# The last two VectorE instructions of a rational activation change places, and one output copy moves up in ScalarE's order

## The chip, the cores and the metric

The kernel runs on one core of a Trainium2 chip. The metric is the device time of one execution in microseconds (us). The five engines of the core are named as in the profile: PE is TensorE's matmul, PEld its weight load, DVE is VectorE, ACT is ScalarE, POOL is GpSimd, and SP (SyncE) issues the DMAs. SBUF is the working memory. [...]

## The reference

Three stages follow each other, all in float32.

```python
# 1. attention with a decaying state, for 4 batches and 8 heads, 768 steps, head size 48
state = alpha[t][:, None] * state + outer(k[t], v[t]);  y[t] = q[t] @ state
# 2. first MoE layer: 3072 tokens, 384 -> 2048 -> 384
h = x @ w_in
P = a[0] + a[1]*h + a[2]*h**2 + a[3]*h**3
Q = 1.0 + |b[0]|*|h| + |b[1]|*h**2
x = (P / (Q + 1e-6)) @ w_out
# 3. second MoE layer, same sizes
h = x @ w_in;  out = (h * cos(h)) @ w_out
```

The change lies in the activation P / (Q + 1e-6) of stage 2, and in the copy that takes attention's output y out of PSUM.

## The kernel before

Attention works in 24 units (6 chunks of 128 time steps by 4 batches), one unit a slot. The first MoE layer is cut into 6 blocks of 512 tokens (`TB`) and 16 slices of 128 hidden channels, so 96 steps `n`; the second layer follows in the same numbering from step 96 on. From slot 20 (`LEAD`) to slot 24 a slot holds one unit of attention and then one step of the layers: `attention(n)`, then `layers(n - LEAD)`, then `y_out(n - 1)`, the copy of attention's output on ACT (line 425). After slot 24 `layers` runs alone.

The whole program stands in a manual schedule: every engine takes its instructions in the order in which the code issues them, and waits only for data and for buffers. A step of `layers(n)` issues these things. `gemm1(n)` (line 562) makes h in a PSUM bank by nine matmuls of 128x512; four banks take turns, so step n needs the bank of step n - 4. `rational(n)` then works on four older steps at once. `second(n)` is `gemm2(n - 5)` (line 578), nine matmuls of 128x512 that read the activation as two parts, `hi` and `lo`.

Inside `rational(n)`, by the age of the step that is worked on:

- step n - 4 (`four`): ACT rounds g to `hi` (line 608), POOL subtracts, lo = g - hi (line 613).
- step n - 2 (`two`): DVE goes on with the numerator, g = (g + a) h (line 628); h is in the PSUM bank. Later ACT writes the logarithm and the exponential of the denominator, thus its reciprocal's first guess r, into the same bank (lines 645 and 646).
- step n - 3 (`three`): DVE runs three instructions. Line 631 makes z = (z + 1.000001) r from SBUF and PSUM. Line 632 writes the corrected r = (z - 2/s) r back into the PSUM bank (the Newton step). Line 633 makes g = (g + c) r from SBUF and PSUM. After line 633 the bank is free for `gemm1`.
- step n - 1 (`one`): ACT makes |h| (line 636) and a h + b (line 637), POOL makes z in two instructions (line 638 with one input in SBUF, line 639 with two), DVE multiplies g by h (line 640).

Beside this, weights and tokens are split into a rounded part and a rest: POOL's line 225 (the rest of a weight), DVE's lines 77 and 78 (weight words), ACT's line 702 and DVE's line 706 (the tokens of the next block, three steps per block; line 706 has both its inputs in SBUF). In DVE's other instructions of the layer one input lies in PSUM.

Of the kernel before, what the change touches and what calls it, by code (L numbers as in the profile page):

```python
# [15 lines left out]
ALU = mybir.AluOpType  # L16
# [15 lines left out]
LN_S = 2.0 ** -22  # L32
# [10 lines left out]
def attn_then_two_moe(ctx, tc, kqT, aT, vP, w1i, w1o, ma, mb, w2i, w2o, out):  # L43
    nc = tc.nc
# [100 lines left out]
    LEAD = NU - 4  # L145
# [268 lines left out]
    def y_out(u):  # L414
        d = U[u]
        if u in late:
            d["yo"] = wp.tile([128, HP, C], F32, tag=late[u], name="yo")
        elif u < NU - B:
            d["yo"] = kept[2 + u % 2]
            if 2 <= u < B:  # L420
                d["yo"] = y_rest[:, (2 + u) * TB:(3 + u) * TB].bitcast(F32).rearrange("p (a t) -> p a t", a=HP)
        else:
            d["yo"] = in_p.tile([128, HP, C], F32, tag="p", name="yo")
        out = d["yo"].bitcast(F32R) if u < B else d["yo"]
        nc.scalar.activation(out=out, in_=d["y"], func=AF.Copy)
# [160 lines left out]
    def acc_out(most=NK):  # L586

        while outs and most:
            most -= 1
            m, blk, f, k = outs.pop(0)  # L590
            ks = slice(k * 128, (k + 1) * 128)
            if f < NF - 1:
                nc.scalar.activation(out=part(blk, k), in_=acc[k], func=AF.Copy)
                continue
            o = temp("z" if k == 1 else "g") if m or blk == NC - 1 else in_p.tile([128, TB], F32, tag="p", name="o")
            if in_parts(m, blk):
                nc.vector.tensor_tensor(out=o, in0=part(blk, k), in1=acc[k], op=ALU.add)
            elif m == 1 and k == 1 and blk in (0, NC - 1):
                nc.vector.tensor_copy(o, acc[k])
            else:  # L600
                nc.scalar.activation(out=o, in_=acc[k], func=AF.Copy)
            to = xd[1][blk, ks, :] if m == 0 else out[ks, blk * TB:(blk + 1) * TB]
            nc.sync.dma_start(out=to, in_=o)

    def round_g(n):
        t = T[n]
        t["hi"] = temp("hi", F32R)
        nc.scalar.activation(out=t["hi"], in_=t["g"], func=AF.Copy)  # L608
# [3 lines left out]
        t["lo"] = temp("lo", F32R)  # L612
        eng.tensor_tensor(out=t["lo"], in0=t["g"], in1=t["hi"].bitcast(F32), op=ALU.subtract)  # L613

    def rational(n):

        def tile_at(i):
            return T[i] if 0 <= i < N1 else None

        one, two, three, four = (tile_at(n - i) for i in range(1, 5))  # L620
        acc_out(1)
        if four:
            round_g(n - 4)
            rest_g(n - 4, nc.gpsimd)
        acc_out()
        if two:
            g = two["g"]
            nc.vector.scalar_tensor_tensor(g, g, cq[:, 3:4], two["h"], ALU.add, ALU.mult)  # L628
        if three:
            z, r, g = three["z"], three["h"], three["g"]  # L630
            nc.vector.scalar_tensor_tensor(z, z, ONE_EPS, r, ALU.add, ALU.mult)  # L631
            nc.vector.scalar_tensor_tensor(r, z, -2.0 / LN_S, r, ALU.add, ALU.mult)
            nc.vector.scalar_tensor_tensor(g, g, cq[:, 2:3], r, ALU.add, ALU.mult)  # L633
        if one:
            h, ah, g, zz = one["h"], temp("ah"), temp("g"), temp("z")
            nc.scalar.activation(out=ah, in_=h, func=AF.Abs)  # L636
            nc.scalar.activation(out=g, in_=h, func=AF.Identity, scale=cq[:, 5:6], bias=cq[:, 4:5])  # L637
            nc.gpsimd.tensor_scalar(zz, ah, cq[:, 1:2], cq[:, 0:1], ALU.mult, ALU.add)  # L638
            nc.gpsimd.tensor_tensor(out=zz, in0=zz, in1=ah, op=ALU.mult)  # L639
            nc.vector.tensor_tensor(out=g, in0=g, in1=h, op=ALU.mult)  # L640
            one.update(z=zz, g=g)
        if two:

            r = two["h"]
            nc.scalar.activation(out=r, in_=two["z"], func=AF.Ln, scale=LN_S, bias=lnb)  # L645
            nc.scalar.activation(out=r, in_=r, func=AF.Exp, scale=-1.0)

    def cosine_parts(n):

        if N1 <= n - 3 < F0:  # L650
            round_g(n - 3)
            rest_g(n - 3, nc.gpsimd)
# [572 lines left out]
        nc.vector.tensor_scalar(bad, tot, 128.0 * 2 * NU - 0.5, None, ALU.is_lt)  # L1225


    def layers(n):
        slot[0] = n + LEAD
        gemm1(n)  # L1230
        if n == F0 - 12:
            all_ok0()
        if n == F0 - 8:
            all_ok1()
        m, r = divmod(n, N1)
        blk, f = divmod(r, NF)
        nxt = (m, blk + 1) if blk + 1 < NC else (m + 1, 0)
        at, load = f - 11, f == 8
        if n < NF:
            nxt, at, load = (0, 1), n - 5, n == 3  # L1240
        elif n < 2 * NF:
            at, load = n - 2 * NF + 4, n == 2 * NF - 6
        split = 0 <= at < NK and nxt[0] < 2 and nxt != (1, 2)
        rational(n)
        cosine_parts(n)
        cosine(n)
        w_hi()
        if split:
            x_hi(*nxt, at)
        second(n)  # L1250
        if 0 < n <= NU - KEEP:
            y_store(KEEP + n - 1)
        if n:
            w_fetch(2 * NF if n < 2 * NF else 3 * NF + NO if n < N1 - NF else 4 * NF)
        if nxt != (1, 2) and load:
            for kk in range(NK):
                x_load(*nxt, kk)
        if split:
            x_lo(*nxt, at)
        i = n - (N1 - NF)  # L1260
        if n < 2 * NF:
            if n > 1:
                tick(2 if n > 4 else 1, 1)
        elif n < N1 - NF:
            if not split:
                tick(1, 1)
        elif n < N1:
            if i > 3:
                tick(1, 1)
        else:  # L1270
            tick(3 if n > N1 + 3 else 1, 1)
        if 0 <= i < NF:
            w_load(i)
        if 0 <= i - 6 < NO:
            w_load(NF + i - 6)
        w_lo([nc.gpsimd])
        if n >= N1:
            now[0] = n - N1 - NF
            prepare(*(SPLIT if split and nxt != (1, 2) else EARLY if now[0] < 0 else PLAIN))
# [7 lines left out]
    with tc.manual_schedule():  # L1287
        nc.scalar.preload_act_table_set("natural_log_exp_and_others")
        for name, u in (("a", 0), ("kq", 0), ("a", 1), ("a", 2), ("kq", 1)):
            load(u, name)  # L1290
        nc.vector.memset(fresh, P_MIN)
        nc.gpsimd.memset(ones, 1.0)
        nc.gpsimd.memset(half_pi, HALF_PI)
        nc.gpsimd.memset(lnb, LN_S * ONE_EPS)
        for t in v_t:
            nc.gpsimd.memset(t[:, H * D:], 0.0)
        nc.gpsimd.memset(ident, 1.0)
        nc.gpsimd.affine_select(
            ident, ident, pattern=[[1, 128]], compare_op=ALU.is_equal, fill=0.0, base=0, channel_multiplier=-1
        )  # L1300
        for s in s_all:
            nc.gpsimd.memset(s[:, HP * D:], 0.0)
        warm_up(13)
        x_pieces = [p for kk in range(NK) for p in x_load(0, 0, kk)]
        for n in range(-3, NU + 1):
            slot[0] = n
            if n == -1:
                load(3, "a")
                load(1, "v")
            if 0 <= n - 2 < KEEP:  # L1310
                y_store(n - 2)
            if 0 <= n - 3 < B:
                y_store(n - 3, True)
            if n >= -1:
                load(n + 5, "a")
            if n >= 0:
                load(n + 3, "kq")
                for i in range(SOME[n] if n <= LEAD else 0):
                    w_fetch(2 * NF)
                load(n + 2, "v")  # L1320
            if n == 3:
                nc.sync.dma_start(out=cab[:, 0:4], in_=ma.unsqueeze(0).to_broadcast([128, 4]))
                nc.sync.dma_start(out=cab[:, 4:6], in_=mb.unsqueeze(0).to_broadcast([128, 2]))
            if n == 6:
                nc.scalar.activation(out=cq[:, 0:2], in_=cab[:, 4:6], func=AF.Abs)
                nc.scalar.activation(out=cq[:, 2:6], in_=cab[:, 0:4], func=AF.Copy, scale=-LN_S * LN_S)
            if n >= 8 and x_pieces:
                x_pieces.pop(0)()
            if n == 1:
                warm_up(8)  # L1330
            attention(n)
            if n == -3:
                for name, u in (("v", 0), ("kq", 2)):
                    load(u, name)
            w_lo([nc.gpsimd])
            if n >= LEAD:
                layers(n - LEAD)
                y_out(n - 1)
        for n in range(NU + 1 - LEAD, F0):
            layers(n)  # L1340
        for k in range(SLOTS):
            threes(k)
        acc_out()
# [183 lines left out]
```

## Time and profile before

| what | value |
|---|---|
| median of 3 runs | 914.39 us (913.3 to 915.9) |
| profiled execution | 913.8 us, its span 912.1 us |
| granted TensorE clock | 0.996 |
| PE busy | 892.4 us (98%) |
| DVE, ACT, POOL busy | 693.9, 697.1, 702.9 us (76 to 77%) |
| attention with layers (slots 20 to 24) | about 98 to 125 us of the span |
| first MoE layer alone | about 125 to 520 us |

"Busy" is time in which an instruction of the engine runs, waits inside an instruction included. Successive instructions of one engine overlap by some hundredths of a microsecond in the records, so the busy time of a full engine comes out slightly above what it occupies.

### The profile page before, as it was taken

What the parts mean: (1) busy time and instruction counts of PE and PEld (TensorE: products, weight loads), DVE (VectorE), ACT (ScalarE), POOL (GpSimd) and SP (SyncE); (2) the same over time, 40 slices, a digit from 0 to 9 for tenths busy, and PEclk for the clock granted to TensorE, in tenths of its full rate; (3) what the DMA queues carried; (4) which work ended last, traced back from release to release, by engine and by line L of the source; (5) the groups of instructions that cost most, each with busy time, mean ns of one, the idle gap of its engine ahead of it and who ended that gap; (6) DMA issues with size and microseconds to landing.
All of it is one profiled execution on the core that took longest, in us unless ns stands there. A gap on an engine that the chain in (4) does not pass through costs nothing.

```text
span 912.1 us, 16494 instructions
## 1 busy us (share of the span) xinstructions
PE 892.4 (98%) x5732; PEld 741.2 (81%) x5732; DVE 693.9 (76%) x1247; ACT 697.1 (76%) x1302; POOL 702.9 (77%) x699
## 2 busy tenths in 40 slices
PE   7999999999999999999999999999999999999997
PEld 7788777887788888888888888878888888888885
DVE  7989799998999989989979767666366554555552
ACT  5999898989889788888788778656577666666653
POOL 6899998999889888889879668669787475655332
PEclk9999999999999999999999999999999999999999
DMA  8999545211233141232165276630243433533432
GB/s 281 357 366 370 191 124 196 82 63 36 104 107 94 57 142 45 87 107 94 53 205 185 95 238 239 202 110 27 74 134 109 161 113 96 167 102 105 139 105 90
DMA packets 67307, 128.87 MB, mean 141 GB/s; under 512 B 6928, under 2 KB 30224, under 8 KB 67216
## 3 DMA queue, kind: packets, MB, share of 16 engines
q1 hardware_dynamic: 67216, 127.74, 43.1%
q8 instruction: 47, 0.77, 0.4%
q14 instruction: 44, 0.36, 0.1%
HBM read 95.21 MB, written 32.51 MB: 140 GB/s over the span
## 4 chain that ended last, share of the span: by engine, by line
PE 72%; DVE 8%; ACT 7%; POOL 6%; DMA 4%; issue 2%; SPq 0%; DVEq 0%; ACTq 0%
PE acc L578 22%; PE b L562 18%; PE acc L1054 15%; PE b L1019 6%; PE r L1019 5%; PE r L562 4%; POOL kq L323 2%; POOL kq L318 2%; DMA kq<-kqT 2%; DVE g L628 1%; DVE z L631 1%; ACT b L645 1%; DVE g L640 1%; DMA a<-aT 1%; PE b L1198 1%
## 5 line engine op out<-in xcount | busy, mean ns | idle before, releaser
L578 PE MATMUL acc<-hi,w 128*128 128x512 f32 x738 | 252.5, 396 | 0.0
L562 PE MATMUL b<-x,w 128*128 128x512 f32 x927 | 233.8, 397 | 1.3 <-DVE g L633 1.1
L613 POOL TENSOR_TENSOR lo<-g,hi 128x512 fp32r<-128x512 f32 x128 | 170.2, 1330 | 66.2 <-ACT hi L608 59.4
L562 PEld LDWEIGHTS b<-x,w 128*128 128x128 f32 x927 | 173.4, 188 | 45.4 <-DVE g L633 4.1
L578 PEld LDWEIGHTS acc<-hi,w 128*128 128x128 f32 x738 | 138.7, 188 | 33.9
L1111 POOL TENSOR_TENSOR lo<-g,hi 128x512 fp32r<-128x512 f32 x64 | 83.0, 1297 | 103.6 <-ACT hi L1110 91.6
L578 PE MATMUL acc<-lo,w 128*128 128x512 f32 x369 | 145.7, 395 | 0.0
L639 POOL TENSOR_TENSOR z<-z,ah 128x512 f32<-128x512 f32 x96 | 124.7, 1299 | 8.0
L1054 PE MATMUL acc<-hi,w_out 128*128 128x512 f32 x384 | 130.3, 395 | 0.0
L608 ACT ACTIVATE hi<-g 128x512 fp32r<-128x512 f32 x128 | 80.4, 628 | 47.8 <-PE acc L578 32.6
L578 PEld LDWEIGHTS acc<-lo,w 128*128 128x128 f32 x369 | 69.4, 188 | 16.5
L638 POOL TENSOR_SCALAR z<-ah,cq 128x512 f32<-128x512 f32 x96 | 74.4, 775 | 5.5 <-ACT ah L636 5.4
L1054 PE MATMUL acc<-lo,w_out 128*128 128x512 f32 x192 | 76.4, 398 | 0.4 <-POOL lo L1111 0.2
L1054 PEld LDWEIGHTS acc<-hi,w_out 128*128 128x128 f32 x384 | 68.7, 188 | 9.9
L640 DVE TENSOR_TENSOR g<-g,b 128x512 f32<-128x512 f32 x72 | 49.1, 682 | 16.2 <-ACT g L637 16.0
L636 ACT ACTIVATE ah<-b 128x512 f32<-128x512 f32 x72 | 42.8, 594 | 19.9 <-PE b L562 19.6
L562 PE MATMUL r<-x,w 128*128 128x512 f32 x225 | 56.8, 397 | 1.0 <-DVE g L633 1.0
L1096 DVE SCALAR_TENSOR_TENSOR ah<-z,b 128x512 f32<-128x512 int32 x44 | 30.2, 685 | 35.9 <-ACT z L1092 35.9
L637 ACT ACTIVATE g<-b,cq 128x512 f32<-128x512 f32 x72 | 56.1, 779 | 0.0
L633 DVE SCALAR_TENSOR_TENSOR g<-g,cq,b 128x512 f32<-128x512 f32 x72 | 53.9, 748 | 2.5
L628 DVE SCALAR_TENSOR_TENSOR g<-g,cq,b 128x512 f32<-128x512 f32 x72 | 53.4, 742 | 0.5
L645 ACT ACTIVATE b<-z,lnb 128x512 f32<-128x512 f32 x72 | 50.1, 696 | 4.7 <-DVE g L628 4.0
(202 smaller groups left out, 2028.7 us busy)
## 6 DMA issues: line engine op xcount, KB each, us to landing
w_out<-wd SPq DMA_DIRECT2D x64, 384.0 KB, 3.1
kq<-kqT SPq DMA_DIRECT2D x24, 512.0 KB, 6.6
w<-wd SPq DMA_DIRECT2D x16, 384.0 KB, 3.1
wd<-w SPq DMA_DIRECT2D x16, 384.0 KB, 2.6
a<-aT SPq DMA_DIRECT2D x23, 258.0 KB, 5.8
raw<-w2o SPq DMA_DIRECT2D x14, 384.0 KB, 3.9
v<-vP SPq DMA_DIRECT2D x24, 192.0 KB, 6.6
x<-x1d SPq DMA_DIRECT2D x18, 256.0 KB, 4.2
```

The costliest lines, as they stand in the source:

```text
L562: nc.tensor.matmul(h, ws[0][f][:, w, ks], x[:, xx, kk, :], start=i == 0, stop=i == 8)
L578: nc.tensor.matmul(acc[k], ws[1][f][:, w, ks], d[g], start=first and i == 0, stop=last and i == 2)
L608: nc.scalar.activation(out=t["hi"], in_=t["g"], func=AF.Copy)
L613: eng.tensor_tensor(out=t["lo"], in0=t["g"], in1=t["hi"].bitcast(F32), op=ALU.subtract)
L628: nc.vector.scalar_tensor_tensor(g, g, cq[:, 3:4], two["h"], ALU.add, ALU.mult)
L638: nc.gpsimd.tensor_scalar(zz, ah, cq[:, 1:2], cq[:, 0:1], ALU.mult, ALU.add)
L639: nc.gpsimd.tensor_tensor(out=zz, in0=zz, in1=ah, op=ALU.mult)
L640: nc.vector.tensor_tensor(out=g, in0=g, in1=h, op=ALU.mult)
L645: nc.scalar.activation(out=r, in_=two["z"], func=AF.Ln, scale=LN_S, bias=lnb)
L1019: nc.tensor.matmul(tile[:, half], w[p], x[q], start=start and i == 0, stop=True, skip_group_check=True)
L1054: nc.tensor.matmul(acc[k], item["w"][:, w, ks], item[g], start=first, stop=last)
L1111: nc.gpsimd.tensor_tensor(out=p["lo"], in0=p["g"], in1=p["hi"].bitcast(F32), op=ALU.subtract)
```

## The change

The Newton factor is no longer multiplied into r in PSUM. Line 632 now makes g = (g + c) r with the uncorrected r, and line 633 multiplies the correction in: g = (z - 2/s) g. The product is the same up to rounding. Line 632 is now the last instruction that reads the bank, and line 633 has both its inputs, z and g, and its output in SBUF.

`layers` and `rational` take an argument `between`, which is called after the instructions on step n - 1 and in front of those on step n - 2 (the logarithm). In slots 20 to 24 `y_out` is passed there; before, it stood behind the whole of `layers`.

```diff
-    def rational(n):
+    def rational(n, between=None):
...
             nc.vector.scalar_tensor_tensor(z, z, ONE_EPS, r, ALU.add, ALU.mult)
-            nc.vector.scalar_tensor_tensor(r, z, -2.0 / LN_S, r, ALU.add, ALU.mult)
             nc.vector.scalar_tensor_tensor(g, g, cq[:, 2:3], r, ALU.add, ALU.mult)
+            nc.vector.scalar_tensor_tensor(g, z, -2.0 / LN_S, g, ALU.add, ALU.mult)
...
             one.update(z=zz, g=g)
+        if between:
+            between()
         if two:
...
-    def layers(n):
+    def layers(n, between=None):
...
-        rational(n)
+        rational(n, between)
...
             if n >= LEAD:
-                layers(n - LEAD)
-                y_out(n - 1)
+                layers(n - LEAD, partial(y_out, n - 1))
```

## Rows read from the trace of the kernel before

**Rows 1.** Page, part 1: busy time, share of the span, instructions.
```profile
PE 892.4 (98%) x5732; PEld 741.2 (81%) x5732; DVE 693.9 (76%) x1247; ACT 697.1 (76%) x1302; POOL 702.9 (77%) x699
```

**Rows 2.** Chain that ended last: start us, us, what; one piece after 244.60 us.
```profile
246.96 2.10 PE acc L578 x9
```

**Rows 3.** Windows: stretch, length, busy time (instructions) of each engine, clock, DMA.
```profile
104.00:125.00 21.00, 19.66 (x213) 15.24 (x210) 15.91 (x27) 19.79 (x40) 20.48 (x23) 1.00 0.50 148
...
120.65:244.60 123.95, 121.72 (x516) 95.65 (x514) 117.31 (x186) 110.75 (x205) 114.15 (x104) 1.00 0.29 90
244.60:510.00 265.40, 265.40 (x1138) 213.86 (x1138) 241.26 (x368) 221.64 (x391) 231.31 (x208) 1.00 0.35 112
```

**Rows 4.** Waits of PE, 100 to 520 us: total us, times, longest.
```profile
PE y L399 <- ACT yo L425: 1.3, 1, 1.3
PE b L562 <- DVE g L633: 1.1, 2, 0.7
```

**Rows 5.** DVE's groups by form: busy us, mean ns, idle before.
```profile
L632 DVE SCALAR_TENSOR_TENSOR b<-z,b 128x512 f32<-128x512 f32 x72 | 50.1, 696 | 2.5
L631 DVE SCALAR_TENSOR_TENSOR z<-z,b 128x512 f32<-128x512 f32 x72 | 48.9, 679 | 0.0
```

**Rows 6.** Single lines 633 and 706: duration ns min/median/max, first and last start.
```profile
L633 DVE SCALAR_TENSOR_TENSOR g<-g,cq,b x72: 746/748/749, 116.9 to 513.3; 128x512 f32<-128x512 f32 x72
...
L706 DVE TENSOR_TENSOR x<-x x21: 683/733/1333, 127.4 to 566.8; 128x512 fp32r<-128x512 f32 x21
```

**Rows 7.** Timeline at 127 us: start us, us, engine, line, out<-in [idle before].
```profile
126.73 1.30 POOL L639 TENSOR_TENSOR z<-z,ah 128x512 f32<-128x512 f32 x1
...
127.44 1.14 DVE L706 TENSOR_TENSOR x<-x 128x512 fp32r<-128x512 f32 x1 [0.58 <-ACT x L702]
...
128.00 1.74 POOL L613 TENSOR_TENSOR lo<-g,hi 128x512 fp32r<-128x512 f32 x1
```

**Rows 8.** POOL's groups from 120.65 to 244.60 us: busy, mean, idle before.
```profile
L613 POOL TENSOR_TENSOR lo<-g,hi 128x512 fp32r<-128x512 f32 x29 | 39.1, 1349 | 6.1 <-ACT hi L608 5.8
L639 POOL TENSOR_TENSOR z<-z,ah 128x512 f32<-128x512 f32 x29 | 37.7, 1299 | 2.4
L638 POOL TENSOR_SCALAR z<-ah,cq 128x512 f32<-128x512 f32 x29 | 22.5, 776 | 0.0
L225 POOL TENSOR_TENSOR w<-st,w 128x384 fp32r<-128x384 f32 x17 | 17.4, 1025 | 0.3 <-ACT w L215 0.3
```

**Rows 9.** Timeline of POOL and DVE, three steps from 186.25 us.
```profile
186.25 1.30 POOL L613 TENSOR_TENSOR lo<-g,hi 128x512 fp32r<-128x512 f32 x1
...
186.98 0.75 DVE L633 SCALAR_TENSOR_TENSOR g<-g,cq,b 128x512 f32<-128x512 f32 x1
...
187.54 0.78 POOL L638 TENSOR_SCALAR z<-ah,cq 128x512 f32<-128x512 f32 x1
...
188.40 1.30 POOL L639 TENSOR_TENSOR z<-z,ah 128x512 f32<-128x512 f32 x1
...
189.97 1.30 POOL L613 TENSOR_TENSOR lo<-g,hi 128x512 fp32r<-128x512 f32 x1 [0.27 <-ACT hi L608]
...
198.72 1.30 POOL L613 TENSOR_TENSOR lo<-g,hi 128x512 fp32r<-128x512 f32 x1
```

**Rows 10.** POOL's groups from 244.60 to 510.00 us: busy, mean, idle before.
```profile
L613 POOL TENSOR_TENSOR lo<-g,hi 128x512 fp32r<-128x512 f32 x64 | 85.7, 1338 | 23.5 <-ACT hi L608 17.0 <-PE acc L578 6.5
...
L638 POOL TENSOR_SCALAR z<-ah,cq 128x512 f32<-128x512 f32 x64 | 49.5, 773 | 5.5 <-ACT ah L636 5.4
L225 POOL TENSOR_TENSOR v<-st,kq 128x384 fp32r<-128x384 f32 x16 | 16.4, 1023 | 0.7
```

**Rows 11.** Timeline of ACT and PE in slots 22 and 23.
```profile
111.13 0.69 ACT L645 ACTIVATE b<-z,lnb 128x512 f32<-128x512 f32 x1 [1.00 <-DVE g L628]
...
113.63 0.59 ACT L425 ACTIVATE yo<-y 128x512 f32<-128x512 f32 x1
...
114.27 1.09 PE L399 MATMUL y<-kq,s 48*64 48x128 f32 x16 [1.34 <-ACT yo L425]
```

## The prediction

> **What bounds the kernel now.** I read the page's busy times first. TensorE is busy for 98% of the span, the other three compute engines for 76 to 77% [rows 1]. That is an average over unlike stages, so the second view was the chain of waits, for the stage that the change touches. From 244.60 us to the end of the first MoE layer the chain holds nothing but TensorE: nine matmuls of gemm1, nine of gemm2, 2.10 us each [rows 2], so 4.20 us a step. The windows confirm it. From 244.60 to 510 us PE is busy all the time (265.40 of 265.40 us), DVE 241.3 and POOL 231.3 [rows 3]. In that stretch neither a bank that comes free sooner nor a shorter VectorE can bring anything; the only question is what spare time the other engines have to lose.
>
> From 120.65 to 244.60 us it is different. There 29 steps (the count of POOL's line 613 [rows 8]) take 123.95 us, 4.27 a step and 2.2 us more than 29 times 4.20. PE stands idle for those 2.2 us [rows 3], partly for the bank that line 633 frees [rows 4]. DVE is busy for 117.3 us and POOL for 114.2 [rows 3]: in this stretch three engines are nearly full, because weights are still converted beside the layer.
>
> **Line 632 and line 633, the gain.** The count of DVE instructions is the same. Before, the bank is free when line 633 ends; after, when line 632 ends, one instruction of 0.70 to 0.75 us earlier [rows 5, 6]. The most that this can return is the PE idle time of the first stretch, 2.2 us; in the second it is worth nothing. The new line 632 no longer needs the result of the instruction in front of it, which may let it start some hundredths sooner. I cost that at nothing, since in the first stretch other things come last.
>
> **Line 633, the price.** Of the five rational instructions that DVE runs in a step, each now has one input in PSUM. The new line 633 has both in SBUF. The trace has one such instruction in this stage, line 706, and its durations are not like the others': line 633 takes 746 to 749 ns in all its 72 rows, line 706 takes 683 at the least and 1333 at the most [rows 6]. The timeline shows why. At 127.44 us line 706 starts while POOL runs line 639; POOL's instruction ends at 128.03, and line 706 ends 0.55 us after that, at 128.58. POOL's next instruction, line 613, starts at 128.00, in the middle of it, and takes 1.74 us where its neighbour takes 1.30 [rows 7]. So the two engines shut each other out: the VectorE instruction waits until POOL's has ended, and POOL's next one is held up by 0.44 us.
>
> [...]
>
> [...]
>
> The change puts this instruction into every one of the 96 steps. In a step POOL runs line 613, line 638 and line 639, and line 225 in 17 of the 29 steps [rows 8]. In the regular part line 633 starts in the middle of POOL's line 613: 186.98 in 186.25 to 187.55 [rows 9]. There is no free place close by, since line 638 follows at 187.54 and line 639 at 188.40.
>
> First stretch, POOL's account. The three steps from 186.25 to 198.72 take 12.47 us. Line 639 of 188.40 ends at 189.70 and line 613 follows at 189.97, which is 0.27 us of idle time [rows 9]; 12.20 are taken. Three of the new holds add 3 x 0.44 = 1.32, together 13.52 us, while PE needs 12.60: POOL becomes the bound, at 4.51 us a step. Over 29 steps that is 130.7 us, 6.8 more than the 123.95 now. This takes for granted that the 2.2 us of stalls, which come in the steps where tokens are split and sums are formed, vanish in the slower pace; if they stay on top it is 8.9. From the other side: 29 holds are 12.8 us, and POOL's usable idle time there is 6.1 + 0.3 = 6.4 us (the 2.4 in front of line 639 are 29 gaps of 0.08 inside a pair, no use to anybody) [rows 8], so +6.4 if all of it is used up and +12.8 if none is. I take +8, near the regular part's account, and keep 6.4 and 12.8 as ends.
>
> Second stretch, the same account. 64 holds are 28.2 us. POOL's usable idle time is 23.5 + 5.5 + 0.7 = 29.7 us [rows 10]. It fits with 1.5 us left, which is to say only just: nothing is lost if every piece of it lies where it is needed, 7 us if a quarter of it doesn't (28.2 - 22.3 = 5.9, and some steps of token splitting, where line 706 competes too). I take +2, nearer to the lower end because PE's queue of four banks evens out a late step here, and keep 0 and +7. DVE has room: 24.1 us idle [rows 3] against waits for POOL of which most steps would have a few tenths.
>
> **The output copy.** In slots 20 to 24 ACT's order changes; no instruction and no DMA is added (the stores of y stand elsewhere in SP's order and wait for the copy alone). In slot 22 ACT idles 1.00 us in front of the logarithm at 111.13, waiting for DVE's line 628, and the copy runs only at 113.63, behind logarithm, exponential and a weight's conversion. PE waits 1.34 us for it, because line 399 writes the same bank [rows 4, 11]. After, the copy falls into the idle 1.00 us, y having been finished before. PE's wait of 1.34 us goes. What is late next is ACT itself: it is busy for 19.79 of the 21 us from 104 to 125 [rows 3], and the 1.00 us is most of what it has free there. So the saving that reaches the layers is the length by which ACT's work moves into the idle time, one copy of 0.59 us at most. In slots 23 and 24 the logarithm comes a copy later, and its reader (line 631) one step later does not wait for it now. Bounds: -1.34 and 0; I take -0.5.
>
> **Sum.** On the profiled execution of 913.8 us: +8, +2, -0.5 and nothing for the bank, since the stalls it would remove are overtaken by POOL's pace: 923.3 us. The median of the runs is 0.6 above the profiled execution; 923.9, so 924 us. The case's own range is 919 to 934: 913.8 and 6.4 + 0 - 1.3 at the bottom, 913.8 and 12.8 + 7 + 0 at the top.
>
> **Rivals.**
>
> A. The bank is what counts. The new line 633 meets no bar, or finds a free place by shifting a few tenths, and the stalls for the bank go: -2.2, with the copy -0.5 to -1.3. That gives 911, on the other side. For it: PE's waits name line 633, and POOL has idle time. Against it: rows 7, and an engine in rows 9 with 0.27 us free in 12.47. It decides from the point where line 633's wait falls below what a step of the first stretch has to spare, (12.60 - 12.47) / 3 = 0.04 us.
>
> B. Only POOL's two-input instructions bar line 633, and line 638 runs beside it. In rows 9 line 633 would then start its work when line 613 ends (187.55) and end 0.55 later at 188.10, where before it ended at 187.73. DVE loses some 0.37 us a step, POOL nothing. DVE's three steps take 12.47 + 1.1 = 13.6 at most, and 12.47 + 0.3 = 12.8 if the earlier start of line 632 and the idle pieces take up most of it: per step 0.06 to 0.33 over 4.20, in the middle 0.15, times 29 = +4.4, with the copy 918.
>
> C. The waits don't settle, and line 633 meets a two-input instruction from its start in every step, the second stretch too: 64 waits of 1.30 are 83 us against DVE's 24 us of idle time, +59, some 973 us. Against it: in rows 7 the waiting instruction got in as soon as POOL's ended, though POOL's next was ready; that pushes POOL back behind line 633 and so breaks the pattern.
>
> D. Waits as forecast, but absorbed: POOL's waits for `hi` (5.8 of its 6.1 us idle) shrink by as much as the holds add, and the steps of token splitting hide the rest. About 914.
>
> **Chances.** Forecast 0.57, A 0.16, B 0.14, D 0.09, C 0.04. A change of less than 0.3% (2.7 us: 911.6 to 917.1) can't be told from none. Slower: the forecast, C, and 0.10 of B make 0.71. Faster: A where the copy gives its full share, 0.11. Same: the rest of A, B and all of D, 0.18. The range from 912 to 934 holds the forecast but for 0.03, B, D and about a third of A, some 0.82.
>
> **What would show it.** Right: line 633's rows spread from under 700 to over 1200 ns; POOL's line 638 or 613 has longer rows behind it; 120 to 245 us grows by some 8 us and PE's idle time there with it, its waits naming `lo` or DVE's line 632; from there on 4.20 us a step nearly throughout; line 399's wait of 1.34 gone. If POOL's line 638 keeps its 0.78 us in rows beside line 633, B holds. If line 633 shows one duration near 0.68, the price was not there and A holds. The forecast fails as a whole if 29 steps of the first stretch take 124 us or less.

## The result, and the profile after

The changed kernel takes 921.4 us (median of 4 runs, 920.5 to 922.4) against 914.3: the ratio is 1.0076, 95% interval 1.0058 to 1.0094. It is slower, as forecast, by about 7 us where the forecast had 10. Its profiled execution took 920.51 us with a span of 918.8.

The page first. VectorE and GpSimd are busy for 26.7 and 42.5 us longer than before [rows 1], with the same number of instructions. POOL's 42.5 us are about 96 times 0.44 (42.2).

```profile
PE 894.3 (97%) x5732; PEld 738.8 (80%) x5732; DVE 720.6 (78%) x1247; ACT 700.1 (76%) x1302; POOL 745.4 (81%) x699
```

Two lines hold that time. Each row below is one line of the changed kernel with its duration in ns (min/median/max).

```profile
L633 DVE SCALAR_TENSOR_TENSOR g<-z,g x96: 692/1020/1820, 116.6 to 524.8; 128x512 f32<-128x512 f32 x96
...
L638 POOL TENSOR_SCALAR z<-ah,cq x96: 766/1209/1287, 106.4 to 518.8; 128x512 f32<-128x512 f32 x96
```

Line 633 had 746 to 749 ns in the 72 rows of [rows 6] (the bank has another name in the other 24 steps, with 747 to 750 ns); now its shortest is 692 and its longest 1820. Line 638 on POOL, which the diff doesn't touch, had a mean of 776 [rows 8] and has a median of 1209. The timeline of the changed kernel shows how the one makes the other:

```profile
186.15 1.29 POOL L613 TENSOR_TENSOR lo<-g,hi 128x512 fp32r<-128x512 f32 x1
186.78 1.21 DVE L633 SCALAR_TENSOR_TENSOR g<-z,g 128x512 f32<-128x512 f32 x1
187.43 1.21 POOL L638 TENSOR_SCALAR z<-ah,cq 128x512 f32<-128x512 f32 x1
...
195.06 1.29 POOL L613 TENSOR_TENSOR lo<-g,hi 128x512 fp32r<-128x512 f32 x1 [0.22 <-ACT hi L608]
```

Line 633 starts in the middle of POOL's line 613, which ends at 187.44; line 633 ends 0.55 us later, at 187.99. POOL's line 638 starts at 187.43, while line 633 still runs, and takes 1.21 instead of 0.77. That is the pair of rows 7, now in most steps: in 80 of its 96 rows line 633 takes over 0.76 us, and in each of these 80 it ends 0.53 to 0.56 us after an instruction of GpSimd. It holds the other way round too, with the instruction that has one input only:

```profile
121.51 0.79 POOL L638 TENSOR_SCALAR z<-ah,cq 128x512 f32<-128x512 f32 x1
121.74 1.09 DVE L633 SCALAR_TENSOR_TENSOR g<-z,g 128x512 f32<-128x512 f32 x1
...
122.38 1.62 POOL L639 TENSOR_TENSOR z<-z,ah 128x512 f32<-128x512 f32 x1
```

Line 638 ends at 122.30, line 633 at 122.83: again half a microsecond behind. Line 639, which starts between them, takes 1.62 us where it had 1.30.

The windows say what this costs, by stretch (columns as in [rows 3]). There the first stretch runs from the first matmul of step 4 (120.65) to that of step 33 (244.60); here these two start at 118.80 and 251.00, so the same 29 steps grew from 123.95 to 132.20 us, and the row goes 0.6 us beyond them.

```profile
118.80:251.60 132.80, 125.35 (x518) 94.94 (x517) 130.35 (x187) 112.55 (x207) 126.96 (x105) 1.00 0.28 86
251.60:517.00 265.40, 265.40 (x1139) 213.85 (x1138) 254.98 (x369) 222.36 (x389) 258.91 (x207) 1.00 0.36 112
```

In the first stretch VectorE and POOL are busy nearly throughout and PE idles for 7.5 us. In the second PE is busy for all of 265.40 us, as before. From the first matmul of step 33 to that of step 127, the last of the second layer, it takes 395.28 us (251.00 to 646.28), and 395.27 before (244.60 to 639.87): the whole loss lies in front of step 33. The chain of waits dates it: the piece that stood at 246.96 us [rows 2] stands at 253.37, 6.4 us later, and from there to the end only 0.3 us are added (918.8 against 912.1).

```profile
251.00 2.37 PE b L562 x9
253.37 2.10 PE acc L578 x9
```

PE's waits now name line 632, which frees the bank (total us, times, longest). The wait of 1.34 us for the output copy [rows 4, 11] is gone.

```profile
PE b L562 <- DVE g L632: 4.7, 12, 0.8
PE r L562 <- DVE g L632: 1.3, 3, 0.6
PE acc L578 <- POOL w L225: 1.3, 1, 1.3
```

### The profile page after: what moved, and what is told of

The parts are those of the page before. It is cut to its first block, busy times and chain, and to the rows that moved or that the text cites. A ratio compares the mean times of both kernels' runs of the same rounds, so it can differ in the third digit from the quotient of the medians.

```text
span 918.8 us, 16494 instructions
## 1 busy us (share of the span) xinstructions
PE 894.3 (97%) x5732; PEld 738.8 (80%) x5732; DVE 720.6 (78%) x1247; ACT 700.1 (76%) x1302; POOL 745.4 (81%) x699
## 3 DMA queue, kind: packets, MB, share of 16 engines
q1 hardware_dynamic: 67216, 127.74, 42.5%
## 4 chain that ended last, share of the span: by engine, by line
PE 72%; DVE 13%; POOL 5%; DMA 4%; ACT 3%; issue 2%; DVEq 0%; SPq 0%; ACTq 0%
PE acc L578 22%; PE b L562 18%; PE acc L1056 15%; PE b L1021 6%; PE r L1021 5%; PE r L562 4%; DVE g L633 2%; DVE g L628 2%; DVE g L632 2%; DVE g L640 2%; DVE z L631 2%; DMA kq<-kqT 2%; POOL kq L323 1%; POOL kq L318 1%; DMA v<-vP 1%
## 5 line engine op out<-in xcount | busy, mean ns | idle before, releaser
L613 POOL TENSOR_TENSOR lo<-g,hi 128x512 fp32r<-128x512 f32 x128 | 181.6, 1419 | 38.4 <-ACT hi L608 38.4
L1113 POOL TENSOR_TENSOR lo<-g,hi 128x512 fp32r<-128x512 f32 x64 | 83.1, 1299 | 103.4 <-ACT hi L1112 91.4
L639 POOL TENSOR_TENSOR z<-z,ah 128x512 f32<-128x512 f32 x96 | 129.8, 1352 | 8.0
L633 DVE SCALAR_TENSOR_TENSOR g<-z,g 128x512 f32<-128x512 f32 x96 | 102.7, 1070 | 3.3
L638 POOL TENSOR_SCALAR z<-ah,cq 128x512 f32<-128x512 f32 x96 | 99.3, 1034 | 0.2 <-ACT ah L636 0.2
L225 POOL TENSOR_TENSOR w<-st,w 128x384 fp32r<-128x384 f32 x48 | 49.8, 1038 | 3.2 <-ACT w L215 3.1
```

Of the source, the lines that this page charges most:

```text
L633: nc.vector.scalar_tensor_tensor(g, z, -2.0 / LN_S, g, ALU.add, ALU.mult)
L1113: nc.gpsimd.tensor_tensor(out=p["lo"], in0=p["g"], in1=p["hi"].bitcast(F32), op=ALU.subtract)
```

## The experiments

The theory under test, P: line 633 with both inputs in SBUF and POOL's instructions shut each other out, and that is the whole loss. Its rivals: C, ScalarE's new order costs the time; O, the order of the three VectorE instructions costs it, whatever memory they use. The first four runs shared one set of runs of the kernel before (914.9 us), the last four another (914.2 us).

**One part at a time.** The new lines 632 and 633 alone, with the copy behind `layers` as before:

```diff
             nc.vector.scalar_tensor_tensor(z, z, ONE_EPS, r, ALU.add, ALU.mult)
-            nc.vector.scalar_tensor_tensor(r, z, -2.0 / LN_S, r, ALU.add, ALU.mult)
             nc.vector.scalar_tensor_tensor(g, g, cq[:, 2:3], r, ALU.add, ALU.mult)
+            nc.vector.scalar_tensor_tensor(g, z, -2.0 / LN_S, g, ALU.add, ALU.mult)
```

> The new arithmetic in lines 632 and 633 alone; the output copy stays behind layers. Theory P (line 633 with both inputs in SBUF and POOL's instructions shut each other out): the whole loss is here and the copy's small gain is missing, 921.8 us, 7.5 above before; line 638 keeps its median near 1.21 us. Theory C (ScalarE's new order costs the time, since the logarithm comes a copy later): 914 us, as before. Theory O (it is the order of the three VectorE instructions, whatever memory they use): 921.8 us too; the run with the product in PSUM tells O from P.

Measured: 920.6 us, ratio 1.0059 (1.0037 to 1.0081), 5.7 us above the kernel before, where P had 7.5. And the copy alone:

```diff
+        if between:
+            between()
...
-                layers(n - LEAD)
-                y_out(n - 1)
+                layers(n - LEAD, partial(y_out, n - 1))
```

> The output copy in its new place alone; lines 632 and 633 as before. Theory P: 913.9 us, 0.4 below before, PE's wait of 1.34 us in front of line 399 gone, ScalarE's idle time in front of the logarithm of slot 22 about 0.5 instead of 1.0 us. Theory C: about 921 us.

Measured: 914.3 us, ratio 0.9991 (0.9973 to 1.0008). The loss is in lines 632 and 633; C falls. What the copy brings can't be told from nothing in these times, but the traces show where it goes. The table has the start of the first matmul of a step (us).

| run | step 0 | step 4 | step 33 | steps 0 to 33 |
|---|---|---|---|---|
| before | 99.08 | 120.65 | 244.60 | 145.52 |
| lines 632 and 633 alone | 98.51 | 120.10 | 250.52 | 152.01 |
| copy alone | 100.77 | 120.78 | 246.11 | 145.34 |
| both | 98.78 | 118.80 | 251.00 | 152.22 |

With the copy alone the wait in front of line 399 is gone and step 4 comes 1.56 us sooner after step 0 (20.01 against 21.57). The very next step gives it back: PE waits 1.43 us for the bank that line 633 frees.

```profile
124.58 2.37 PE L562 MATMUL b<-x,w 128*128 128x512 f32 x9 [1.43 <-DVE g L633]
```

At step 33 0.2 us of it are left. With the new lines alone the loss up to step 33 is 6.5 us, with the copy beside them 6.7.

**The same order, one input in PSUM.**

```diff
-            nc.vector.scalar_tensor_tensor(g, g, cq[:, 2:3], r, ALU.add, ALU.mult)
-            nc.vector.scalar_tensor_tensor(g, z, -2.0 / LN_S, g, ALU.add, ALU.mult)
+            nc.vector.scalar_tensor_tensor(r, g, cq[:, 2:3], r, ALU.add, ALU.mult)
+            nc.vector.scalar_tensor_tensor(g, z, -2.0 / LN_S, r, ALU.add, ALU.mult)
```

> Both parts of the change, in the new order of the arithmetic, but line 632 writes its product into the PSUM bank and line 633 reads it there: no VectorE instruction of the step has two inputs in SBUF, and the bank is free after line 633 as before. Theory P: 913.5 us (913 to 914.3), line 633 in one duration near 0.70 us in all its rows, line 638 back at 0.77 us. Theory O: about 921 us.

Measured: 913.7 us, ratio 0.9978 (0.9966 to 0.9990): as fast as P has it. Its two lines (ns min/median/max):

```profile
L633 DVE SCALAR_TENSOR_TENSOR g<-z,b x72: 686/687/691, 117.2 to 511.9; 128x512 f32<-128x512 f32 x72
...
L638 POOL TENSOR_SCALAR z<-ah,cq x96: 762/777/802, 107.1 to 507.8; 128x512 f32<-128x512 f32 x96
```

Line 633 is back to one duration and line 638 to its own. Only the place of the product differs from the changed kernel, and with it the instruction that frees the bank: it is free an instruction later here, and yet the kernel is faster. Against the kernel before the gain is 0.2%. That is no more than the two sets of runs of that kernel differ by (914.9 and 914.2 us), so whether this version beats it as well is not settled.

**The old order, both inputs in SBUF.**

```diff
-            nc.vector.scalar_tensor_tensor(g, g, cq[:, 2:3], r, ALU.add, ALU.mult)
-            nc.vector.scalar_tensor_tensor(g, z, -2.0 / LN_S, g, ALU.add, ALU.mult)
+            nc.vector.scalar_tensor_tensor(z, z, -2.0 / LN_S, r, ALU.add, ALU.mult)
+            nc.vector.scalar_tensor_tensor(g, g, cq[:, 2:3], z, ALU.add, ALU.mult)
```

> Both parts, but the arithmetic in the old order: line 632 corrects r first, and writes it over z in SBUF, not into the bank; line 633 then multiplies (g + c) by it, with both inputs in SBUF. The bank is free after line 632, as in the changed kernel. Theory P: the loss is that of the changed kernel, 921 us within 1.5, line 633 spread from 0.75 to 1.8 us and line 638's median near 1.2. Theory O (the order of the arithmetic): 914.

Measured: 924.6 us, ratio 1.0107 (1.0091 to 1.0122). O falls: the old order loses as well once line 633 has two inputs in SBUF. It loses 3 us more than P said, which is outside the expectation. The starts of the steps say where. Up to step 28 this run and the changed kernel are level (129.53 and 129.47 us from step 0 to step 28). From step 29 to step 33, where tokens are split and sums are formed, this run takes 21.52 us (234.87 to 256.39) and the changed kernel 17.63 (233.37 to 251.00). Line 633 has five rows in these steps. Here four of them are held, in the changed kernel none (first this run's row, then the changed kernel's: total us, mean ns):

```profile
L633 DVE SCALAR_TENSOR_TENSOR g<-g,cq,z 128x512 f32<-128x512 f32 x5 | 7.0, 1402 | 0.2
```

```profile
L633 DVE SCALAR_TENSOR_TENSOR g<-z,g 128x512 f32<-128x512 f32 x5 | 3.6, 725 | 0.2
```

That is 3.4 us more in line 633, by the same exclusion. From step 33 on PE is busy throughout here too:

```profile
256.39:510.00 253.61, 253.61 (x1085) 203.92 (x1086) 241.67 (x350) 211.40 (x371) 242.96 (x195) 1.00 0.35 110
```

Why the holds fall into these steps here is not shown. One difference that could move them: in this order each of the three instructions needs the result of the one in front of it, and line 632 starts 0.71 us after line 631 (182.21 and 182.92) where the changed kernel has 0.60 (185.40 and 186.00).

**The new pair in steps 33 to 95 only.**

```diff
+            if n - 3 >= 33:
+                nc.vector.scalar_tensor_tensor(g, g, cq[:, 2:3], r, ALU.add, ALU.mult)
+                nc.vector.scalar_tensor_tensor(g, z, -2.0 / LN_S, g, ALU.add, ALU.mult)
+            else:
+                nc.vector.scalar_tensor_tensor(r, z, -2.0 / LN_S, r, ALU.add, ALU.mult)
+                nc.vector.scalar_tensor_tensor(g, g, cq[:, 2:3], r, ALU.add, ALU.mult)
```

> Both parts, but the new lines 632 and 633 are used only from step 33 of the first layer on (63 of 96 steps); steps 0 to 32 keep the old pair. Theory P with the two accounts of the prediction (the first 29 full steps pay, from 245 us on POOL's idle time takes the holds): 914 us within 1 us, line 633 in these steps still spread from 0.69 to 1.8 us. If each such instruction costs its share wherever it stands: 63/96 of 7.1, 918.5 us. Theory O: as the latter.

Measured: 914.4 us, ratio 0.9979 (0.9965 to 0.9992). In 63 of the 96 steps the new instruction costs nothing. It is held there (its row, ns min/median/max; line 634 in this kernel), and PE's window is full all the same:

```profile
L634 DVE SCALAR_TENSOR_TENSOR g<-z,g x63: 692/883/1783, 258.3 to 518.4; 128x512 f32<-128x512 f32 x63
```

```profile
246.00:510.00 264.00, 264.00 (x1133) 212.68 (x1133) 250.59 (x365) 220.95 (x387) 252.35 (x205) 1.00 0.35 110
```

**The new pair in one of three steps, steps 0 to 32 only.**

```diff
+            if n - 3 < 33 and n % 3 == 0:
...
+            else:
...
```

> Both parts, but the new lines 632 and 633 only in every third of the first 33 steps (11 of 96). POOL's account of the prediction: three steps take 12.20 + 0.44 = 12.64 us against PE's 12.60, so next to nothing is lost: 914.5 us within 1. If every such instruction in the first stretch costs its share of the 7.5 us, a third: 916.5.

Measured: 915.6 us, ratio 1.0018 (1.0008 to 1.0028). That lies between the two expectations, and the time doesn't decide. The trace bears out the account for the regular part: three steps of POOL take 12.56 and 12.53 us, under PE's 12.60, and only the one line 638 (642 in this kernel) that follows the new instruction is longer.

```profile
181.80 1.28 POOL L613 TENSOR_TENSOR lo<-g,hi 128x512 fp32r<-128x512 f32 x1
183.07 1.20 POOL L642 TENSOR_SCALAR z<-ah,cq 128x512 f32<-128x512 f32 x1
...
194.36 1.29 POOL L613 TENSOR_TENSOR lo<-g,hi 128x512 fp32r<-128x512 f32 x1
...
206.89 1.29 POOL L613 TENSOR_TENSOR lo<-g,hi 128x512 fp32r<-128x512 f32 x1
```

In 143 to 224 us PE is busy throughout, as before. What is lost shows behind it, where tokens are split and sums are formed. There PE is busy for 20.17 of 22 us, and 20.86 in the kernel before. The first row is this run's, the second the kernel's before.

```profile
224.00:246.00 22.00, 20.17 (x84) 15.11 (x83) 21.65 (x33) 16.79 (x30) 19.65 (x17) 1.00 0.17 57
```

```profile
224.00:246.00 22.00, 20.86 (x87) 15.74 (x86) 21.61 (x34) 17.61 (x31) 19.20 (x17) 1.00 0.21 70
```

Two accounts fit. Before, three steps of POOL took 12.47 us [rows 9], so it gained 0.13 on PE each time and met that part with a lead; at 12.55 it hardly gains any. And the token instruction, which has two inputs in SBUF in both kernels, is held in all three of its rows there (1.19, 1.06 and 1.19 us), where before it took 0.73, 1.07 and 0.69; the new pair stands there once, and isn't held (0.69 us at 234.94). Which of the two costs the time is not told apart.

**Freeing the bank sooner in another way.** Line 628 behind the three instructions on step n - 3, once with the pair of the kernel before and once with the product in PSUM, both with the copy in its new place:

```diff
-        if two:
-            g = two["g"]
-            nc.vector.scalar_tensor_tensor(g, g, cq[:, 3:4], two["h"], ALU.add, ALU.mult)
         if three:
...
+        if two:
+            g = two["g"]
+            nc.vector.scalar_tensor_tensor(g, g, cq[:, 3:4], two["h"], ALU.add, ALU.mult)
```

> A way to free the bank sooner without two inputs in SBUF: old lines 631 to 633, but line 628 (the work on step n - 2) is issued behind them, and the copy in its new place. The bank comes free 0.66 us sooner in VectorE's order; the logarithm, which waits for line 628, comes some 2.1 us later in the step. If the stalls for the bank (2.2 us in the first stretch) were all that is left, 912.5; if ScalarE, held at the logarithm, brings the rounding of the next step late, 914 to 918. I expect 914.

> The run with the product in PSUM, and line 628 behind the three instructions on step n - 3. If the bank alone makes the stalls that are left, 912.5, a microsecond below the run with the product in PSUM; if the logarithm's delay counts, 914 to 918. I expect 913.5.

Measured: 972.1 us (ratio 1.0628, 1.0612 to 1.0644) and 960.0 us (1.0505, 1.0489 to 1.0521), both far outside what I expected. ScalarE's longest waits in the first of the two (total us, times, longest; line 633 is line 628 moved) and VectorE's first instruction in two following steps:

```profile
ACT b L647 <- DVE g L633: 65.4, 47, 3.2
ACT r L647 <- DVE g L633: 16.7, 12, 1.9
```

```profile
304.06 0.69 DVE L628 SCALAR_TENSOR_TENSOR z<-z,b 128x512 f32<-128x512 f32 x1 [0.91 <-ACT b L648]
...
308.43 0.69 DVE L628 SCALAR_TENSOR_TENSOR z<-z,b 128x512 f32<-128x512 f32 x1 [0.31 <-ACT b L648]
```

These two steps start 4.37 us apart, over PE's 4.20. I had counted the logarithm's delay and missed that it closes a loop. The logarithm and the exponential of a step wait for the moved instruction, and the next step's first VectorE instruction waits for the exponential, so the four VectorE instructions and the two of ScalarE follow each other. At 0.17 us a step this loop makes some 16 of the 58 us. The other steps are longer: 5.20 us on the average from step 4 to step 33 (119.79 to 270.57). There a weight's words stand in the loop as well: ScalarE's line 73 comes behind the logarithm, VectorE's line 77 waits for it, and the next step's first instruction stands behind line 77.

```profile
200.33 0.56 DVE L77 SCALAR_TENSOR_TENSOR r<-st,r 128x384 int32<-128x384 int32 x1 [2.10 <-ACT r L73]
200.80 0.68 DVE L628 SCALAR_TENSOR_TENSOR z<-z,b 128x512 f32<-128x512 f32 x1
```

So these two runs don't tell what a bank that is free sooner would be worth by itself.

## Why the prediction was right

Point by point, in the order of its steps.

- **The mechanism.** Right. Line 633's spread, the 0.55 us behind POOL's instruction and the 0.44 us by which POOL's next one grows are those of rows 7, and taking the second SBUF input away takes the loss away, with the order left as it is (913.7 us against 921.4).
- **Line 638, the open price.** The prediction left it open between its forecast and rival B. The forecast's 0.44 us a step supposes that line 638, which follows line 633 in the regular part, is held as line 613 is in rows 7; no row of the kernel before shows that. The changed kernel does: POOL's one-input instruction blocks line 633 (which ends 0.53 us behind it, at 122.83) and is blocked by it (1.21 us in the median for 0.77, 0.44 longer); rival B, which had it run beside, is out.
- **First stretch, +8.** Too high: it measured 6.5 us with the new lines alone, next to the lower end of 6.4. In the changed kernel the 29 steps grew by 8.25 us, but 1.55 of that is the copy's gain given back. POOL's account was a little low for the regular part: it gave 13.52 us for three steps, and the trace has 13.74 (from 181.32 to 195.06), the difference being 0.22 us of waiting for `hi` that I had counted as used up. The steps with token splitting made up for it: steps 29 to 33 took 17.63 us and 17.97 before (226.63 to 244.60), and line 633 was not held there. That was luck, and the run with the old order, held in these steps, shows it was worth over 3 us.
- **POOL as the bound.** Argued, not shown. VectorE has no idle time in the regular part either, since it waits inside line 633, and POOL's 0.22 us for `hi` hang on VectorE: ScalarE's rounding (194.37) stands behind its line 73, which waits 2.08 us for VectorE's line 78. The runs don't tell which of the two engines sets the pace.

```profile
193.91 0.52 ACT L73 ACTIVATE r<-raw 128x384 int32<-128x384 uint8 x1 [2.08 <-DVE st L78]
```

- **Second stretch, +2 of 0 to 7.** The mechanism was right and the size was 0. Of POOL's usable 29.7 us of idle time [rows 10] the changed kernel leaves 1.0 + 0.2 = 1.2 us, where the account said 1.5; the pieces lay where they were needed. The run with the new pair in late steps alone shows it by itself. The prediction's three terms of +8, +2 and -0.5 came out as about 6.5, 0 and 0; this is the distance from 924 to 921.4. (POOL's groups from 252 to 517 us, with 63 rows of line 613 and not 64.)

```profile
L613 POOL TENSOR_TENSOR lo<-g,hi 128x512 fp32r<-128x512 f32 x63 | 95.4, 1514 | 1.0 <-ACT hi L608 1.0
...
L638 POOL TENSOR_SCALAR z<-ah,cq 128x512 f32<-128x512 f32 x64 | 63.2, 988 | 0.2 <-ACT ah L636 0.2
L225 POOL TENSOR_TENSOR v<-st,kq 128x384 fp32r<-128x384 f32 x16 | 19.1, 1192 | 0.0
```

- **The output copy, -0.5.** The copy moved where it was expected and PE's wait went, but not the time: what it saved came back one step later as a wait for the bank, and 0.2 us or nothing is left (table above). The prediction looked for what is late next in ScalarE, and it was the bank. In the changed kernel it runs in front of the logarithm, in the time in which ScalarE was idle:

```profile
109.75 0.60 ACT L425 ACTIVATE yo<-y 128x512 f32<-128x512 f32 x1
110.87 0.69 ACT L647 ACTIVATE b<-z,lnb 128x512 f32<-128x512 f32 x1 [0.52 <-DVE g L628]
```

- **The bank, nothing.** Right in this kernel. The bank is free an instruction sooner, but that instruction is itself later, and PE waits more for it than it did before: 4.7 and 1.3 us, against 1.1 [rows 4] and 1.0 for the bank named r, whose row is this:

```profile
PE r L562 <- DVE g L633: 1.0, 1, 1.0
```

So nearly all of PE's 2.2 us before were waits for the bank, where the prediction said partly.

- **Rivals.** A had the bank decide; the run with the product in PSUM frees the bank as late as before and has the lowest median of all. C's endless pattern didn't come: a waiting line 633 got in when POOL's instruction ended, as at 187.44 us with line 638 ready. D, absorption, holds in the second stretch and fails in the first, where POOL still had 3.5 us of waits for `hi` and PE waited for the bank.

## What to carry to other kernels

In this kernel VectorE's line 633 with both inputs in SBUF takes as long as with one in PSUM (692 ns at the least, and 686) only where it isn't held: in 80 of 96 rows it waits for GpSimd's instruction, ending 0.53 to 0.56 us behind it after up to 1820 ns, and GpSimd's line 638 takes 1.21 us in the median for 0.77. Before moving a product from PSUM to SBUF to free a bank, add the holds to GpSimd's account in the stretch where it is fullest, and compare with its usable idle time there; an average over the kernel would have hidden it (76% and 77% busy). Leave a few microseconds on either side, because the holds can fall into the steps that have no room: in steps 29 to 33 four of five rows were held with the old order and none with the new, 3.4 us of line 633, and what moved them is not shown. And a bank that is waited for can be worth less than the order that frees it (PE waited 2.2 us here, and moving line 628 cost 46 and 58): look for the loop that a moved instruction closes.

## What the runs showed of the hardware beyond the expectation

The exclusion is as strong for GpSimd's one-input line 638 as for its two-input line 613: line 638 grew from 0.77 to 1.21 us, by the same 0.44 us as line 613 in rows 7 (1.74 for 1.30). Line 633 without a per-partition scalar operand is also the shorter one with an input in PSUM: 687 ns for line 633 with the product in PSUM, against 748 with the operand `cq` in the kernel before [rows 6]. It is so with both inputs in SBUF too: the shortest row of line 633 is 692 ns in the changed kernel, without `cq`, and 751 in the run with the old order, with it. So the new line's 0.05 us comes from the operand (59 and 60 ns between the shortest rows) and not from the memory (5 and 6 ns).
